# Chunks 0 to 3 of a retention kernel: scaled values, a mask made on the chip, and another order of loads

## The chip, the cores and the metric

One core of a Trainium2 chip runs one program. The metric is the device time of one execution in microseconds (us), as the median of several runs. The profile is one execution with every instruction, semaphore and DMA recorded. TensorE (PE in the profile) multiplies; PEld is its weight load. VectorE is DVE, ScalarE is ACT, GpSimd is POOL. SyncE (SP) only issues DMAs.

## The reference, cut to what matters

Three stages follow one another: retention (a linear attention with decay), a first MLP, and an RMS norm with a gated MLP. Only retention is touched by most of the change.

```
state = gamma * state + k[t]^T v[t]          # per batch and head, 64 x 64
y[t]  = 1/sqrt(64) * q[t] state              # q, k, v: (2, 8, 768, 64)
h = x @ w_in;  x2 = (h * sigmoid(1.702 h)) @ w_out            # (1536, 512), d_ff 2048
xn = x2 / rms(x2) * rms_g;  out = (silu(xn @ w_gate) * (xn @ w_val)) @ w_out2
```

`gamma` is 1 - 2^(-5 - head). `w_in`, `w_out` and the other weights arrive as 64-bit floats and are converted on the chip.

## The kernel before, in words

**Tiles.** The 768 positions of a batch are six chunks of 128, so there are twelve chunks; `CPB` is 4, the chunks of one block of 512 tokens. Tokens are worked through in three blocks of 512. Chunks 0 to 3 are the first block; they are done in an opening that is written out by hand (lines 850 to 965). Chunks 4 to 11 run inside the loop over the sixteen column blocks f of the first MLP (lines 1002 to 1052).

**A chunk.** `score_products` makes k q for all eight heads (two PSUM tiles, even and odd heads). `masks` multiplies them on VectorE with `dm_sb`, a loaded table that holds scale * gamma^(t-s) on and above the diagonal and zero elsewhere. `intra` multiplies the values with the masked scores. `inter` multiplies the state of the chunks before with q times a decay (`prep_q`, on GpSimd, with the loaded table `qd_sb`) into the same PSUM tile y. `update_products` multiplies k times a decay (`prep_k`, on GpSimd, with `sm_sb`) with the values; `decay` (ScalarE) and `add_update` (VectorE) make the next state S. `x_high` (ScalarE) and `x_low` (VectorE) store y as a rounded part and the rest; the MLP's products use three products of such parts (high x high, high x low, low x high).

**Weights.** `load_next` brings half a weight block (512 KB) into one of four buffers; `convert` turns it into 32-bit floats in five steps, which the opening calls one by one as r[0] to r[4] (ScalarE, ScalarE, VectorE, VectorE, VectorE or the end); `split_in` and `split_out` make the high and low parts. `in_proj` makes h of one column block in twelve products of 512 columns; in the opening h0 is made in two groups, 384 columns for chunks 0 to 2 and 128 for chunk 3 (lines 940 and 952). `mlp1_act` is the gate, on ScalarE, with its low part on VectorE.

**What sets the order.** In the opening, `in_order` pins each engine's instructions to the order of the text. Behind it a planner orders each engine's instructions by its own costs, program order being the priority, and may draw instructions forward into the opening. SyncE issues loads in the order of the text (lines 866 to 886); two small ones go out on ScalarE's queue (`sm_sb`, line 871, and `g_sb`, line 882, the norm's factor, which ScalarE later scales on line 1076).

**Near the end of the first MLP**, `set_tasks` gives five steps that make the seven operands of the next stage's products out of a weight block (x, sums, more, y, z); at f = 14 one of them is called for block 0 (line 1024), the others at f = 15.

Of the kernel before, what the change touches and what calls it, by code (L numbers as in the profile page):

```python
# [19 lines left out]
C = 128  # L20
# [7 lines left out]
T = 512  # L28
# [16 lines left out]
HELD = 2  # L45
WARM, MORE = 8, 0
# [7 lines left out]
def tile_retention_mlp_swiglu(  # L54
# [231 lines left out]
    def prep_k(c):  # L286
        t = tmp(f"kd{c}")
        nc.gpsimd.tensor_tensor(
            out=t.rearrange("p (h d) -> p h d", h=H),
            in0=ld["kv", c][:, 0],  # L290
            in1=sm_sb[:, 0:H].to_broadcast([128, H, D]),
            op=ALU.mult,
        )
        at["kd", c] = t
# [17 lines left out]
    def score_products(c, p):  # L312
        t = ld["qk", c]
        sc = at["sc", c] = [psum(p, f"sc{c}_{e}") for e in range(2)]
        begun = len(nc.cur_bb.bb.instructions)
        earlier = of(mybir.EngineType.PE)[-1]
        for n in range(NP):
            for e in range(2):
                nc.tensor.matmul(  # L319
                    out=sc[e][:, n * C:(n + 1) * C],  # L320
                    lhsT=t[64 * e:64 * e + 64, 1, n, :],
                    rhs=t[64 * e:64 * e + 64, 0, n, :],
                    start=True,
                    stop=True,
                )
        if c > CPB:
            after(of(mybir.EngineType.PE, begun)[0], earlier)

    def masks(c):
        sc = at.pop(("sc", c))  # L330
        for e in range(2):
            a = tmp(f"a{c}_{e}")
            nc.vector.tensor_tensor(
                out=a, in0=sc[e], in1=dm_sb[:, e].rearrange("p n c -> p (n c)"), op=ALU.mult
            )
            at["a", c, e] = a
# [11 lines left out]
    def inter(c, p):  # L348
        if c % NC == 0:
            return  # L350
        y, begins = y_of(c, p)
        qd = at.pop(("qd", c))
# [25 lines left out]
    def x_of(c):  # L378
# [8 lines left out]
        return [x[:, :, i * C:(i + 1) * C] for x in xt[j]]  # L387

# [478 lines left out]
    load_mask(0)  # L867
    load_qk(1)
    load_mask(1)
    load_kv(0)  # L870
    nc.scalar.dma_start(out=sm_sb.rearrange("p n o -> p (n o)"), in_=small)
    load_kv(1, (1,))
    nc.sync.dma_start(out=qd_sb.rearrange("p n c -> p (n c)"), in_=qdec)
    load_qk(2)
    load_kv(1, (0,))
    load_kv(2)
    load_qk(3)
    load_next()
    load_kv(3)
    for _ in range(3):  # L880
        load_next()
    nc.scalar.dma_start(out=g_sb, in_=rms_g)
    load_qk(CPB)
    load_kv(CPB)
    load_qk(CPB + 1)
    load_kv(CPB + 1)

    nc.scalar.activation(out=first, in_=ones[:, 0:1], func=ACTF.Silu)
    score_products(0, ps_a)
    score_products(1, ps_a)  # L890
    warming(MORE)
    masks(0)
    prep_k(0)
    intra(0, ps_h)
    masks(1)
    x_high(0)
    intra(1, ps_h)
    update_products(0, ps_t)
    prep(1)
    add_update(0)  # L900
    x_low(0)
    decay(1)

    score_products(2, ps_a)
    inter(1, ps_h)
    update_products(1, ps_t)
    masks(2)
    prep(2)
    x_high(1)
    add_update(1)  # L910
    x_low(1)
    r = convert_next(split=True)
    decay(2)
    r[0]()
    r[1]()

    intra(2, ps_h)
    score_products(3, ps_a)
    masks(3)
    r[2]()  # L920
    inter(2, ps_h)
    update_products(2, ps_t)
    add_update(2)
    prep(3)
# [6 lines left out]
    decay(3)  # L931
    r = convert_next(split=True)
    r[0]()
    r[2]()
    intra(3, ps_h)
    inter(3, ps_h)
    x_high(3)
    ps = psum(ps_a, "h0")
    w = parts.pop(("wi", 0))
    in_proj(ps, w, xt[0], True, 0, T - C)  # L940
    update_products(3, ps_t)
    x_low(3)
    r[1]()
    r[3]()
    r[4]()
    load_next()
    add_update(3)
# [3 lines left out]
    split_in(1)  # L951
    in_proj(ps, w, xt[0], True, T - C, T)
    score_products(CPB, ps_t)
    r[2]()
    r[3]()
    ready = of(mybir.EngineType.DVE)[-1]
    masks(CPB)
    prep_q(CPB)
    tc.add_manual_dep(of(mybir.EngineType.Pool)[-1], ready.name, WAIT, reason="order of issue")
# [42 lines left out]
    for f in range(1, F1):  # L1002
# [14 lines left out]
        if f == F1 - 2:  # L1017
# [6 lines left out]
            some(sets[0], 1)  # L1024
# [349 lines left out]
```

## Time and profile before

| | |
|---|---|
| median of 3 runs | 585.38 us (585.36 to 585.67) |
| the profiled execution | 585.22 us |
| its span, first to last instruction | 583.4 us |
| TensorE busy | 575.7 us (99%) |
| VectorE busy | 450.7 us (77%) |
| ScalarE busy | 365.4 us (63%) |
| GpSimd busy | 24.5 us (4%) |
| granted TensorE clock | 0.999 |
| DMA | 135.11 MB, mean 232 GB/s |

The chain of waits that ended last is made of TensorE to 97% and of DMA to 2%. Busy time of TensorE counts from the first to the modelled end of pipelined products, so a busy TensorE is not one at its peak. A row's idle time stands in brackets with what ended it.

### The profile page before, as it was taken

The page shows a single profiled execution, that of the slowest core. Times are in us where ns is not written, and L with a number is a line of the kernel's source. Part 1 is how long each engine was busy: PE and PEld are TensorE (multiplying, and loading weights), DVE is VectorE, ACT ScalarE, POOL GpSimd, SP SyncE. Part 2 cuts the span into 40 slices and gives each one's busy share as a digit, 9 for nine tenths or more (in the row PEclk, how much of TensorE's full clock was granted, in tenths as well). Part 3 has the DMA queues.
Part 4 walks back from the last instruction along what each step waited for, and adds up shares of the span by engine and source line. Part 5 has one row for each costly group of instructions (what it writes and reads, how often), then busy time and mean ns, then how long its engine had stood idle before and what let it go on. Part 6 is the DMA issues. An engine that isn't in the chain of part 4 may idle for free.

```text
span 583.4 us, 9280 instructions
## 1 busy us (share of the span) xinstructions
PE 575.7 (99%) x3274; PEld 481.1 (82%) x3274; DVE 450.7 (77%) x806; ACT 365.4 (63%) x697; POOL 24.5 (4%) x26
## 2 busy tenths in 40 slices
PE   7999999999999999999999999999999999999997
PEld 5887887888788888878888888988989889988885
DVE  3899998879989888367998998888958676644542
ACT  2878776667687887466647875666645446634442
POOL 3300212100000000000000000000000000000000
PEclk9999999999999999999999999999999999999999
DMA  8999999888369899878744336676414476560412
GB/s 321 408 287 379 391 325 370 276 258 311 115 238 317 285 328 349 306 246 315 290 162 165 108 122 203 200 230 220 163 61 138 145 273 247 201 207 11 152 65 74
DMA packets 48287, 135.11 MB, mean 232 GB/s; under 512 B 5616, under 2 KB 5872, under 8 KB 48240
## 3 DMA queue, kind: packets, MB, share of 16 engines
q1 hardware_dynamic: 47808, 134.37, 66.0%
q8 instruction: 26, 0.43, 0.3%
q14 instruction: 21, 0.17, 0.1%
q10 hardware_dynamic: 432, 0.14, 0.1%
HBM read 98.84 MB, written 35.65 MB: 231 GB/s over the span
## 4 chain that ended last, share of the span: by engine, by line
PE 97%; DMA 2%; ACT 0%; DVE 0%; issue 0%; ACTq 0%
PE acc L444 8%; PE h L467 8%; PE acc L446 7%; PE acc L445 7%; PE o L444 6%; PE o L445 6%; PE o L446 6%; PE sc L319 2%; PE y L356 2%; PE y L369 2%; DMA qk<-in_qk 1%; PE m7a L778 1%; PE v0a L778 1%; PE m0a L778 1%; PE m1a L778 1%; PE g10a L778 1%
## 5 line engine op out<-in xcount | busy, mean ns | idle before, releaser
L445 PE MATMUL o<-w,gh 128*128 128x512 f32 x144 | 56.2, 390 | 0.0
L444 PE MATMUL o<-w,gh 128*128 128x512 f32 x144 | 56.2, 390 | 0.0
L446 PE MATMUL o<-w,gl 128*128 128x512 f32 x144 | 56.1, 389 | 0.0
L201 DVE CUSTOM_DVE_ANT_0 qw<-qw,uw 128x1024 uint16<-128x1024 uint16 x67 | 45.9, 686 | 2.6 <-ACT uw L199 0.5
L198 ACT ACTIVATE qw<-w 128x512 f32<-128x512 f32 x67 | 44.6, 665 | 2.6 <-DMA w<-in_w 2.6
L199 ACT ACTIVATE uw<-w 128x512 uint32<-128x512 uint32 x67 | 44.7, 668 | 0.0
L450 DVE TENSOR_TENSOR gl<-gw,gh 128x512 fp32r<-128x512 f32 x24 | 16.6, 691 | 27.1 <-ACT gh L449 27.0
L200 DVE TENSOR_SCALAR qw<-qw 128x512 uint32<-128x512 uint32 x67 | 28.8, 431 | 9.9 <-ACT qw L198 9.8
L449 ACT ACTIVATE gh<-gw 128x512 fp32r<-128x512 f32 x24 | 15.1, 630 | 28.0 <-PE o L445 22.5
L446 PEld LDWEIGHTS o<-w,gl 128*128 128x128 f32 x144 | 27.0, 188 | 5.7
L445 PEld LDWEIGHTS o<-w,gh 128*128 128x128 f32 x144 | 27.1, 188 | 4.6
L444 PEld LDWEIGHTS o<-w,gh 128*128 128x128 f32 x144 | 27.1, 188 | 4.5
L444 PE MATMUL acc<-gh,wo 128*128 128x512 f32 x64 | 25.9, 412 | 0.0
L446 PE MATMUL acc<-gh,wo 128*128 128x512 f32 x64 | 25.0, 391 | 0.0
L445 PE MATMUL acc<-gl,wo 128*128 128x512 f32 x64 | 25.0, 391 | 0.0
L445 PE MATMUL acc<-gl,wowp 128*128 128x512 f32 x64 | 24.9, 389 | 0.0
L446 PE MATMUL acc<-gh,wowp 128*128 128x512 f32 x64 | 24.9, 389 | 0.0
L444 PE MATMUL acc<-gh,wowq 128*128 128x512 f32 x64 | 24.9, 389 | 0.0
L445 PE MATMUL acc<-gl,wowq 128*128 128x512 f32 x64 | 24.9, 389 | 0.0
L446 PE MATMUL acc<-gh,wowq 128*128 128x512 f32 x64 | 24.9, 389 | 0.0
L207 DVE SCALAR_TENSOR_TENSOR qw<-w,qw 128x512 uint32<-128x512 uint32 x36 | 24.7, 686 | 0.2
L467 PE MATMUL h<-xt0h,wih 128*128 128x512 f32 (+2 forms) x68 | 24.8, 387 | 0.0
(1519 smaller groups left out, 1691.4 us busy)
## 6 DMA issues: line engine op xcount, KB each, us to landing
w<-in_w SPq DMA_DIRECT2D x68, 512.0 KB, 6.2
qk<-in_qk SPq DMA_DIRECT2D x12, 512.0 KB, 7.6
kv<-in_kv SPq DMA_DIRECT2D x10, 512.0 KB, 8.5
gmd<-gm SPq DMA_DIRECT2D x16, 256.0 KB, 4.4
gwm<-gmd SPq DMA_DIRECT2D x16, 256.0 KB, 4.5
g1d<-gs SPq DMA_DIRECT2D x12, 256.0 KB, 2.1
g2d<-gl SPq DMA_DIRECT2D x12, 256.0 KB, 2.6
gw<-g1d SPq DMA_DIRECT2D x12, 256.0 KB, 3.4
```

Source lines behind the costliest of these rows:

```text
L198: lambda: nc.scalar.activation(out=q, in_=high.bitcast(F32), func=ACTF.Copy, scale=2.0 ** -112),
L199: lambda: nc.scalar.activation(out=t, in_=low, func=ACTF.Copy, scale=2.0 ** -29),
L200: lambda: nc.vector.tensor_scalar(out=m, in0=m, scalar1=3, scalar2=None, op0=ALU.logical_shift_left),
L201: lambda: nc.vector.tensor_tensor(out=m, in0=m, in1=t, op=ALU.add),
L207: nc.vector.scalar_tensor_tensor(out=dst, in0=high, scalar=0x80000000, in1=m, op0=ALU.bitwise_and, op1=ALU.bitwise_or)
L444: nc.tensor.matmul(out=out, lhsT=ah, rhs=bh, start=first, stop=False)
L445: nc.tensor.matmul(out=out, lhsT=ah, rhs=bl, start=False, stop=False)
L446: nc.tensor.matmul(out=out, lhsT=al, rhs=bh, start=False, stop=last)
L449: nc.scalar.activation(out=hi, in_=src, func=ACTF.Copy)
L450: nc.vector.tensor_tensor(out=lo, in0=src, in1=hi.bitcast(F32), op=ALU.subtract)
L467: nc.tensor.matmul(out=ps[:, begin:end], lhsT=w[a][:, k * 128:(k + 1) * 128], rhs=x[b][:, k, begin:end], start=begin == 0 and o == order[0 ...
L778: nc.tensor.matmul(out=bank, lhsT=u, rhs=v, start=first and k == 0 and x == 0, stop=k == 1 and x == 2, skip_group_check=True,)
```

## The change

For chunks 0 to 3 the decay is taken apart differently. `prep_k` scales the values instead of k, by gamma^(127 - s), and both `update_products` (k unscaled, values scaled) and `intra` use the scaled values. The mask is then gamma^(-128) per head on and above the diagonal and zero elsewhere: `steps`, filled by eight VectorE fills and two GpSimd selects in a buffer that a later tile of x uses. What is left, scale * gamma^(t+1), is `qd_sb`: for chunks 0 and 1 y is multiplied with it on VectorE before x is taken (`scale_y`), and q is used as loaded; for chunks 2 and 3 q is multiplied with it before the scores, and the same q is used for scores and state.

Other parts: for chunks 0 and 3 three of eight heads of the scaled values are made on ScalarE; the scores of chunk 0 go to four PSUM tiles and are masked in halves; the mask table `dm_sb` is loaded in one piece behind chunk 4's q and k; k and v of chunks 0 to 3 are loaded apart, v first; `g_sb` is loaded last, from SyncE; h0 is made in one group of twelve; `in_proj` takes low weights before low x where it goes by part; the order of the opening is new; at f = 14 three steps of block 0 are called, not one.

```diff
+BY_Y = 2
-    def prep_k(c):
+    def prep_k(c, end=H):
         t = tmp(f"kd{c}")
         nc.gpsimd.tensor_tensor(
-            in0=ld["kv", c][:, 0],
-            in1=sm_sb[:, 0:H].to_broadcast([128, H, D]),
+            out=t.rearrange("p (h d) -> p h d", h=H)[:, 0:end],
+            in0=ld["kv", c][:, int(c < CPB), 0:end],
+            in1=sm_sb[:, 0:end].to_broadcast([128, end, D]),
             op=ALU.mult,
         )
+        for h in range(end, H):
+            nc.scalar.activation(out=t[:, o], in_=ld["kv", c][:, 1, h, :], func=ACTF.Copy, scale=sm_sb[:, h, :])
     def score_products(c, p):
+        q = t[:, 0] if c < BY_Y or c >= CPB else at["qd", c].rearrange("p (n c) -> p n c", n=NP)
+        sc = at["sc", c] = [psum(p, f"sc{c}_{e}") for e in range(2 if c else 4)]
     def masks(c):
+        table = steps if c < CPB else dm_sb
+        step = T if c else T // 2
+        for x, o in enumerate(range(0, T, step)):
+            for e in range(2):
+                nc.vector.tensor_tensor(out=at["a", c, e][:, o:o + step], in0=sc[2 * x + e][:, o:o + step], ...
     def inter(c, p):
+        qd = ld["qk", c][:, 0].rearrange("p n c -> p (n c)") if c < BY_Y else at.pop(("qd", c))
     def intra(c, p):
+                    lhsT=at["kd", c][:, (2 * n + e) * D:(2 * n + e) * D + D] if c < CPB else ld["kv", c][:, 1, 2 * n + e, :],
+    def scale_y(c):
+        t = tmp(f"ys{c}")
+        nc.vector.tensor_tensor(out=t, in0=at["y", c], in1=qd_sb.rearrange("p n c -> p (n c)"), op=ALU.mult)
+        at["y", c] = t
     def update_products(c, p):
+        if c < CPB:
+            kd, vt = ld["kv", c][:, 0].rearrange("p h d -> p (h d)"), kd
     def in_proj(ps, w, x, by_part, begin=0, end=T):
-            order.sort(key=lambda o: (0, 2, 1)[o[1]] if begin == 0 and end < T else o[1])
+            order.sort(key=lambda o: (0, 2, 1)[o[1]])
+    steps = xt_p.tile([128, 2, NP, C], F32, tag="xt1h", name="steps")
+    for e in range(2):
+        for n in range(NP):
+            nc.vector.memset(steps[:, e, n, :], (1.0 - 2.0 ** (-5.0 - (2 * n + e))) ** -C)
+        nc.gpsimd.affine_select(
+            out=steps[:, e], in_=steps[:, e], pattern=[[0, NP], [1, C]], compare_op=ALU.is_ge,
+            fill=0.0, base=0, channel_multiplier=-1,
+        )
```

The new order of loads on SyncE (`sm_sb` alone stays on ScalarE's queue): q and k of 0, q and k of 1, v of 0, v of 1, k of 0, `qd_sb`, q and k of 2, k of 1, q and k of 3, v of 2, k of 2, v of 3, first weights, k of 3, second weights, q and k of 4, `dm_sb`, third and fourth weights, then chunks 4 and 5, `g_sb`.

The new order of the opening, where a name stands for the function and its chunk:

```
scores 0 (ps_a), scores 1 (ps_t), masks 0, prep_k 0 (5 heads on GpSimd), intra 0, masks 1, prep_k 1, update 0,
intra 1, add_update 0, scale_y 0, x_high 0, x_low 0, prep_q 2, decay 1, inter 1, update 1,
scores 2, scale_y 1, add_update 1, prep_q 3, prep_k 2, x_high 1, masks 2, x_low 1, decay 2,
inter 2, scores 3, intra 2, update 2, prep_k 3 (5 heads), masks 3, convert r[0..2], add_update 2, r[3..4], load,
x_high 2, split_in 0, x_low 2, intra 3, inter 3, convert r[0], x_high 3, x_low 3, update 3, h0 (twelve products),
r[1], r[2], decay 3, r[3], add_update 3, r[4], load, split_in 1, convert r[0..1],
scores 4, masks 4, prep_q 4, r[2..4], load, gate of h0, prep_k_by_head 4, split_out 0
```

```diff
@@ f == F1 - 2
-            some(sets[0], 1)
+            some(sets[0], 3)
```

## Rows read from the trace of the kernel before

**Rows 1.** Busy time by stretch: start:end length, PE, PEld, DVE, ACT, POOL, clock, DMA share, GB/s
```profile
4.41:29.40 24.99, 22.23 (x293) 19.07 (x293) 17.03 (x30) 14.75 (x38) 9.54 (x8) 1.00 1.02 399
29.40:60.00 30.60, 30.60 (x240) 24.79 (x240) 28.65 (x52) 25.02 (x50) 2.34 (x2) 1.00 0.97 339
60.00:137.50 77.50, 77.50 (x560) 62.63 (x559) 67.29 (x110) 54.26 (x103) 12.15 (x9) 1.00 0.93 325
...
145.00:160.00 15.00, 15.00 (x67) 11.86 (x66) 14.92 (x24) 10.67 (x18) 0.00 (x0) 1.00 0.35 125
```

**Rows 2.** Timeline of TensorE, opening: start, us, line, operation, [idle before <- what ended it]
```profile
4.41 1.55 PE L319 MATMUL sc<-qk 64*128 64x128 f32 x16
7.25 1.16 PE L319 MATMUL sc<-qk 64*128 64x128 f32 x16 [1.30 <-DMA qk<-in_qk]
8.71 1.10 PE L369 MATMUL y<-a,kv 128*64 128x128 f32 x16 [0.29 <-DVE a L333]
10.05 1.09 PE L369 MATMUL y<-a,kv 128*64 128x128 f32 x16 [0.24 <-DMA kv<-in_kv]
...
12.01 1.16 PE L319 MATMUL sc<-qk 64*128 64x128 f32 x16 [0.40 <-DMA qk<-in_qk]
...
18.93 1.09 PE L369 MATMUL y<-a,kv 128*64 128x128 f32 x16 [0.52 <-DVE S_sb L429]
```

**Rows 3.** Chain of waits, the products of h0 (two groups) and h1: start, us
```profile
21.05 2.28 PE h L467 x12
23.95 1.49 PE h L467 x12
...
26.52 2.94 PE h L467 x12
```

**Rows 4.** Timeline of VectorE in the opening
```profile
6.01 0.69 DVE L333 TENSOR_TENSOR a<-sc,dm_sb 128x512 f32<-128x512 f32 x1 [6.01 <-PE sc L319]
...
11.65 0.42 DVE L431 COPY S_sb<-u 128x256 f32<-128x256 f32 x1 [1.78 <-PE u L413]
```

**Rows 5.** Timeline of GpSimd in the opening
```profile
0.73 0.20 POOL L851 MEMSET ones<- 128x128 f32 x1 [0.29 <-POOLq L1367]
...
9.37 1.04 POOL L288 TENSOR_TENSOR kd<-kv,sm_sb 128x512 f32<-128x512 f32 x1 [8.36 <-DMA kv<-in_kv]
10.65 1.27 POOL L281 TENSOR_TENSOR qd<-qk,qd_sb 128x512 f32<-128x512 f32 x1 [0.24 <-DMA qd_sb<-in_qdec]
12.61 1.04 POOL L288 TENSOR_TENSOR kd<-kv,sm_sb 128x512 f32<-128x512 f32 x1 [0.68 <-DMA kv<-in_kv]
...
18.95 1.43 POOL L288 TENSOR_TENSOR kd<-kv,sm_sb 128x512 f32<-128x512 f32 x1 [1.84 <-DMA kv<-in_kv]
```

**Rows 6.** Timeline of ScalarE in the opening
```profile
6.12 0.21 ACT L1076 ACTIVATE g_sb<-g_sb 128x4 f32<-128x4 f32 x1 [2.77 <-DMA g_sb<-in_rms_g]
...
25.47 0.60 ACT L494 ACTIVATE g<-h 128x512 f32<-128x512 f32 x1 [0.60 <-PE h L467]
...
26.64 2.01 ACT L300 ACTIVATE kd<-kv,sm_sb 128x64 f32<-128x64 f32 x8
```

**Rows 7.** Timeline of VectorE behind the opening
```profile
33.70 0.68 DVE L450 TENSOR_TENSOR wil<-w,wih 128x512 fp32r<-128x512 f32 x1
...
45.10 0.69 DVE L488 SCALAR_TENSOR_TENSOR gl<-g,gh 128x512 fp32r<-128x512 f32 x1
```

**Rows 8.** Timeline of ScalarE behind the opening
```profile
38.93 0.66 ACT L198 ACTIVATE qw<-w 128x512 f32<-128x512 f32 x1 [1.01 <-DMA w<-in_w]
...
43.41 0.58 ACT L494 ACTIVATE g<-h 128x512 f32<-128x512 f32 x1
```

**Rows 9.** Timeline of TensorE behind the opening
```profile
35.22 0.39 PE L467 MATMUL h<-xt0h,wil 128*128 128x512 f32 x1
...
37.26 0.39 PE L467 MATMUL h<-xt0h,wil 128*128 128x512 f32 x1
...
46.72 0.39 PE L445 MATMUL acc<-gl,wo 128*128 128x512 f32 x1
```

More of the change, by code (lines that the diff above doesn't have):

```diff
@@ L313, in score_products @@
         t = ld["qk", c]
-        sc = at["sc", c] = [psum(p, f"sc{c}_{e}") for e in range(2)]
+        q = t[:, 0] if c < BY_Y or c >= CPB else at["qd", c].rearrange("p (n c) -> p n c", n=NP)
+        sc = at["sc", c] = [psum(p, f"sc{c}_{e}") for e in range(2 if c else 4)]
         begun = len(nc.cur_bb.bb.instructions)
@@ L319, in score_products @@
                 nc.tensor.matmul(
-                    out=sc[e][:, n * C:(n + 1) * C],
+                    out=sc[e if c else n // 2 * 2 + e][:, n * C:(n + 1) * C],
                     lhsT=t[64 * e:64 * e + 64, 1, n, :],
-                    rhs=t[64 * e:64 * e + 64, 0, n, :],
+                    rhs=q[64 * e:64 * e + 64, n, :],
                     start=True,
@@ L330, in masks @@
         sc = at.pop(("sc", c))
+        table = steps if c < CPB else dm_sb
         for e in range(2):
[L332 to L336, printed above, removed]
+            at["a", c, e] = tmp(f"a{c}_{e}")
+        step = T if c else T // 2
+        for x, o in enumerate(range(0, T, step)):
+            for e in range(2):
+                nc.vector.tensor_tensor(
+                    out=at["a", c, e][:, o:o + step],
+                    in0=sc[2 * x + e][:, o:o + step],
+                    in1=table[:, e].rearrange("p n c -> p (n c)")[:, o:o + step],
+                    op=ALU.mult,
+                )
     def scores(c, p):
@@ L875, in tile_retention_mlp_swiglu @@
     load_kv(1, (0,))
-    load_kv(2)
     load_qk(3)
+    load_kv(2, (1,))
+    load_kv(2, (0,))
+    load_kv(3, (1,))
     load_next()
-    load_kv(3)
-    for _ in range(3):
+    load_kv(3, (0,))
+    load_next()
+    load_qk(CPB)
+    nc.sync.dma_start(out=dm_sb.rearrange("p e n c -> p (e n c)"), in_=dmask)
+    for _ in range(2):
         load_next()
-    nc.scalar.dma_start(out=g_sb, in_=rms_g)
-    load_qk(CPB)
     load_kv(CPB)
@@ L886, in tile_retention_mlp_swiglu @@
     load_kv(CPB + 1)
+    nc.sync.dma_start(out=g_sb, in_=rms_g)
     nc.scalar.activation(out=first, in_=ones[:, 0:1], func=ACTF.Silu)
     score_products(0, ps_a)
-    score_products(1, ps_a)
+    score_products(1, ps_t)
     warming(MORE)
     masks(0)
-    prep_k(0)
+    prep_k(0, 5)
     intra(0, ps_h)
     masks(1)
+    prep_k(1)
+    update_products(0, ps_a)
+    intra(1, ps_h)
+    add_update(0)
+    scale_y(0)
     x_high(0)
[L897 to L900, printed above, removed]
     x_low(0)
+    prep_q(2)
     decay(1)
+    inter(1, ps_h)
+    update_products(1, ps_a)
     score_products(2, ps_a)
-    inter(1, ps_h)
-    update_products(1, ps_t)
+    scale_y(1)
+    add_update(1)
+    prep_q(3)
+    prep_k(2)
+    x_high(1)
     masks(2)
-    prep(2)
-    x_high(1)
-    add_update(1)
     x_low(1)
+    decay(2)
+    inter(2, ps_h)
+    score_products(3, ps_a)
+    intra(2, ps_h)
+    update_products(2, ps_t)
+    prep_k(3, 5)
+    masks(3)
     r = convert_next(split=True)
-    decay(2)
     r[0]()
     r[1]()
-    intra(2, ps_h)
-    score_products(3, ps_a)
-    masks(3)
     r[2]()
-    inter(2, ps_h)
-    update_products(2, ps_t)
     add_update(2)
-    prep(3)
     r[3]()
@@ L930, in tile_retention_mlp_swiglu @@
     x_low(2)
-    decay(3)
+    intra(3, ps_h)
+    inter(3, ps_h)
     r = convert_next(split=True)
     r[0]()
-    r[2]()
[L935 to L943, printed above, removed]
+    x_high(3)
+    x_low(3)
+    update_products(3, ps_t)
+    ps = psum(ps_a, "h0")
+    in_proj(ps, parts.pop(("wi", 0)), xt[0], True)
+    r[1]()
+    r[2]()
+    decay(3)
     r[3]()
+    add_update(3)
     r[4]()
     load_next()
-    add_update(3)
+    split_in(1)
     r = convert_next(split=True)
@@ L950, in tile_retention_mlp_swiglu @@
     r[1]()
-    split_in(1)
-    in_proj(ps, w, xt[0], True, T - C, T)
     score_products(CPB, ps_t)
+    masks(CPB)
+    prep_q(CPB)
     r[2]()
     r[3]()
[L956 to L959, printed above, removed]
     r[4]()
```

17 lines of the change are left out of this document (7 added, 10 removed).

## The prediction

> **What bounds the kernel now.** I read the busy time by stretch first [rows 1], then TensorE's own timeline of the opening [rows 2], then the engines that feed it [rows 4 to 6], and last the first iterations behind the opening [rows 7 to 9]. The reader is to see in the stretches that from 29.40 us on TensorE is busy for all of 30.60, 77.50 and 15.00 us: nothing stands open there, and a feeder that gets faster behind 29.4 us can give nothing. Between 4.41 and 29.40 us it is busy for 22.23 of 24.99 us. This is the only place that the change can shorten; what it does elsewhere can only cost.
>
> The open time of the opening is in five gaps [rows 2]: 1.30 us until chunk 1's q and k land, 0.29 us until chunk 0's masked scores are there, 0.24 us for chunk 1's values, 0.40 us for chunk 2's q and k, 0.52 us for the state S that chunk 2's update makes. Sum 2.75 us.
>
> Two feeders are nearly full: DMA has a share of 1.02 in the opening and 0.97 from 29.4 to 60 us, and VectorE is busy for 28.65 of 30.60 us there [rows 1]. So a TensorE that is earlier by x meets weights that are not earlier by x. That decides how much of x is kept.
>
> **The change, part by part.** *Landings.* All loads go down one line, and a wait that a load ends tells when it was there. Counted in KB from the line's start: 1,280 (chunk 1's q, k) at 7.25 us [rows 2]; 2,048 (chunk 0's k) at 9.37 and 2,560 (the q decay) at 10.65 [rows 5]; 2,304 at 10.05 and 3,072 at 12.01 [rows 2]; 3,328 at 12.61 and 5,376 (chunk 3's k, v) at 18.95 [rows 5]. From 1,280 to 3,328 KB that is 5.36 us, or 0.67 us for 256 KB. The new line has the same bytes in another order. Chunk 1's q, k are complete at 1,024 KB: 7.25 - 0.67 = 6.6 us. Then v of chunk 0 (1,280 KB, 7.25), v of 1 (7.9), k of 0 (8.6), q decay (9.3), q, k of 2 (10.65), k of 1 (11.3), q, k of 3 (12.6), v of 2 (13.3), k of 2 (13.9), v of 3 (14.6), first weights (15.9), k of 3 (16.6), second weights (5,376 KB, 18.95). The mask table lands behind chunk 4's q, k at 21.6 us (two times 512 KB, 2.68 us, on) and is first read behind 24 us. The third weights go back by one such place, to 23.0 us; by the list below ScalarE reads them from 23.3 us, so I cost that at nothing, with 0.3 us of cover.
>
> *Triangle.* Eight fills of 128 columns on VectorE and two selects of 512 columns on GpSimd, ahead of the first scores. No row shows either. A VectorE copy of 256 columns took 0.42 us [rows 4] and a GpSimd fill of 128 columns 0.20 us [rows 5], so I take 0.25 us a fill: four are done at 1.75 us, eight at 2.75. A select lies between that 0.20 us and the 1.43 us of the longest GpSimd product of 512 columns; I take 1.04 us, its usual time [rows 5]. The selects end at 2.8 and 3.9 us, at the upper bound at 4.6 us. The masks want them at 5.2 us, half way through the first scores. Cost nothing; what happens without that cover is a rival below.
>
> [...]
>
> *Chunk 0.* The first scores still run from 4.41 to 5.96 us. The second start at 6.6 instead of 7.25 and end at 7.75 (1.16 us). The first a x v product has a new wait: beside the masked scores it now needs scaled values, five heads on GpSimd (5/8 of 1.04 = 0.65 us) and three on ScalarE (2.01/8 = 0.25 us each [rows 6]) from 7.25 us: ready at 8.05 us. It had started at 8.71. All of TensorE is queued behind it, so this wait carries the whole advance. The masks of chunk 0, four halves of 0.42 us from 5.2 us, are done at 6.9 and lie beside it.
>
> Gaps so far: 5.96 to 6.6 (0.64) and 7.75 to 8.05 (0.30).
>
> *Chunks 1 to 3.* From 8.05 us I put the products one behind the other in the new order and look for what is late. Update 0 at 9.1 needs k of 0 (8.6). a x v of chunk 1 at 9.7 needs its scaled values (GpSimd 7.95 to 9.0) and masks (9.1). Its state product at 10.7 needs S, copied at 10.2. Update 1 at 11.75 needs k of 1 (11.3): 0.45 us to spare, the tightest load. Scores 2 at 12.35, state product 2 at 13.45 (S at 13.2), scores 3 at 14.5, a x v 2 at 15.55 (scaled values 14.8, masks 14.9), update 2, a x v 3 at 17.2 (masks 16.95), state product 3 at 18.25, update 3 at 19.3 to 19.85. None is late by this list, so the gaps 0.24, 0.40 and 0.52 go too. Two multiplications of y on VectorE (0.69 us each, as the masks) and the longer split masks (4 x 0.42 against 2 x 0.69) add 1.7 us to VectorE, and six heads 1.5 us to ScalarE; until 16 us both had long idle stretches (VectorE 1.78 us before the copy at 11.65 [rows 4]), so I cost them at nothing. GpSimd loses one product of 1.27 us [rows 5].
>
> *h0 in one group.* It must wait for chunk 3's x. y of chunk 3 ends at 19.3; ScalarE has one step of the second weights (there at 18.95) ahead of it, so with 0.60 us for each of the two [rows 6] x is there at 20.15: a new gap of 0.30 us. In return twelve products of 512 columns take 2.94 us, as h1 does, where the two groups took 2.28 and 1.49 us [rows 3]: 0.83 us less.
>
> *Sum of the opening:* 2.75 - (0.64 + 0.30 + 0.30) + 0.83 = 2.34 us. The scores of chunk 4, which followed h0 at 25.44 us (23.95 + 1.49), would start near 23.1. Bounds: 3.58 us with no gap at all (2.75 + 0.83); and 0.58 us if the scaled values took 1.43 us, the longest GpSimd product, in place of 0.65, and h0's weights slipped by 0.98 us more, as the load at 18.95 did against the 0.67 us pace (12.61 + 5.36 = 17.97).
>
> *What the feeders let through.* ScalarE's gate for h0 ran at 25.47 us [rows 6]. In the new order it has ahead of it, from 20.15 us: a step of the second weights (0.6), four state decays (1.0), VectorE's signs of those weights (0.7), their split (0.6) and two steps of the third weights (1.2), and so comes at 24.3 to 24.6. It and VectorE are thus earlier by about 0.9 us, not 2.34, and both are full from there on. Iteration 2's low weights were done at 34.38 us (33.70 + 0.68) [rows 7] and read at 35.22 [rows 9], 0.84 us to spare. New: ready 33.5, wanted 32.9. TensorE gives 0.6 us back: 2.34 - 0.6 = 1.7 us kept.
>
> *The last edit* takes four 256-column sums of VectorE (0.42 us each) one iteration earlier, near 130 us. TensorE has no gap there, so it gains nothing. VectorE is busy for 14.92 of 15.00 us from 145 to 160 us [rows 1]; its bound is a loss of 1.7 us if all four stood ahead of something awaited, and I take zero, since they leave the later, fuller stretch.
>
> The profiled execution had 585.22 us, span 583.4, so 1.8 us lie around the span; the median of the runs is 585.38. Span 581.7, executions 583.5, and beside the median 585.38 - 1.7 = **583.7 us**.
>
> **Rivals.** *A, the old order of ScalarE holds.* In iteration 2 the gate of h2 (its last product ended at 37.65 us [rows 9]) ran only at 43.41 us, behind work that began when a weight load landed at 38.93 [rows 8]; its low part was there at 45.79 (45.10 + 0.69) [rows 7], wanted at 46.72 [rows 9]. The line of loads has the same bytes before that load, so it is not earlier. If the gate stays behind it, only 46.72 - 45.79 = 0.93 us is kept: 584.45 us. For it: DMA share 0.97 there. Against it: that order is the planner's, and with h2 earlier the gate can move ahead.
>
> *B, slower: the norm factor's scaling stands in ScalarE's way.* Its load goes from ScalarE's queue (landed 6.1 us) to the end of SP's, behind chunk 5's k, v: 8,960 KB, or 18.95 + 14 x 0.67 = 28.3 us. The scaling was drawn forward into the opening, where ScalarE stood 2.77 us for it [rows 6]. If the planner puts it before the gate of h0 at 24.6, ScalarE stands for 3.7 us, iteration 2's weights come at 37.2 instead of 33.5, and TensorE wants them at 32.9: 2.34 - 4.3 = -2.0, or 587.4 us. From a stand of about 1.7 us on it decides against the kernel. For it: it happened before; against it: behind 25 us ScalarE has other work ready.
>
> *C, late triangle.* If the second select ends at X, behind 7.3 us, GpSimd's scaled values follow at X + 0.65 and the first a x v product at X + 0.7, in place of 8.05. At X = 9.9 that is 10.6, 2.55 us later, and all of the 2.34 us is gone: 585.6 us. It needs selects of 3.6 us each (9.9 less 2.75, halved), against 1.43 us for the longest product [rows 5]. [...]
>
> *D, all is kept:* the planner moves the low weights of iteration 2 forward too: 585.38 - 2.34 = 583.04 us.
>
> **Chances.** Forecast 0.40 (own range 583.0 to 584.2), A 0.25, B 0.12, C 0.08, D 0.10; 0.05 for a late load somewhere in chunks 1 to 3, which takes about 2 us, to 585.7. What a measurement of this kernel can tell from no change is 0.2%, or 1.17 us: below 584.21 lie the forecast and D, 0.50; above 586.55 lies B and a tail of C and the last case, 0.17; between them 0.33. From 582.8 to 586.6 us leaves out about 0.17 above and little below.
>
> **What would show it.** The first a x v product near 8.05 us and waiting for GpSimd or ScalarE, not for VectorE; TensorE's gaps from 4.4 to 23 us near 1.2 us in sum; twelve h0 products in a row from about 20.15; scores of chunk 4 near 23.1. A gap of some 0.6 us before iteration 2's low-weight products shows the forecast, one near 45 us A; a ScalarE idle until 28 us at the g_sb scaling shows B; a first mask behind 7 us shows C. I am wrong if the opening itself does not get shorter, or if TensorE stands open anywhere behind 60 us.

## The result and the profile after

The changed kernel is slower: 590.19 us (median of 17 runs, 588.51 to 591.11) against 585.65 us for the kernel before beside it (17 runs). The ratio is 1.0057, with a 95% interval of 1.0036 to 1.0077; the medians alone stand 4.54 us or 0.8% apart. The kernel before has a few single runs at 589 to 593 us in each comparison, which enter its ratios and not its median, so the medians are given with each ratio below. The forecast of 583.7 us and its range of 582.8 to 586.6 us both miss. The profiled execution took 591.01 us, with a span of 588.2 us and a mean granted clock of 0.997.

Busy time by stretch of the changed kernel, with the columns of [rows 1]:

```profile
4.41:29.40 24.99, 22.05 (x280) 18.18 (x280) 18.45 (x31) 14.00 (x37) 7.31 (x7) 1.00 1.01 391
29.40:60.00 30.60, 30.50 (x237) 24.13 (x237) 28.93 (x53) 26.37 (x53) 4.19 (x2) 1.00 0.90 326
60.00:90.00 30.00, 30.00 (x226) 24.31 (x225) 26.35 (x41) 20.70 (x45) 5.97 (x4) 1.00 0.95 332
90.00:105.00 15.00, 12.76 (x101) 10.18 (x102) 13.00 (x20) 9.84 (x20) 2.57 (x2) 0.89 0.94 324
105.00:145.00 40.00, 40.00 (x254) 32.58 (x251) 33.04 (x54) 26.59 (x48) 3.79 (x3) 1.00 0.86 293
145.00:160.00 15.00, 14.87 (x65) 11.59 (x64) 13.94 (x23) 11.13 (x20) 0.00 (x0) 1.00 0.42 145
```

Two things are to be seen. The opening is no fuller than before (22.05 of 24.99 us). And from 90 to 105 us, where the kernel before had no gap, TensorE is busy for only 12.76 of 15 us and its clock is 0.89.

**The opening.** TensorE's timeline there (start, us, line, operation, what ended the idle time before it), to be held against [rows 2]:

```profile
7.73 1.09 PE L382 MATMUL y<-a,kd 128*64 128x128 f32 x16 [0.63 <-POOL kd L289]
...
13.50 1.09 PE L369 MATMUL y<-qd,S_sb 64*64 64x128 f32 x16 [0.32 <-DVE S_sb L449]
...
18.79 1.09 PE L369 MATMUL y<-qd,S_sb 64*64 64x128 f32 x16 [0.57 <-DVE S_sb L449]
...
21.71 1.20 PE L487 MATMUL h<-xt0h,wih 128*128 128x512 f32 x4 [1.22 <-ACT xt0h L408]
...
24.82 1.52 PE L326 MATMUL sc<-qk 64*128 64x128 f32 x16
26.45 1.21 PE L487 MATMUL h<-xt0h,wih 128*128 128x512 f32 x4
```

The first a x v product is a whole 0.98 us earlier than in [rows 2]. But four gaps (0.63 + 0.32 + 0.57 + 1.22 = 2.74 us) have taken the place of five with 2.75. Chunk 4's scores start at 24.82 us, 0.54 us earlier than the 25.36 us of the kernel before, and h1 starts at 26.45 us in both: by the end of the opening nothing is gained.

**The stall.** TensorE around chunk 9, with the last product ahead of the gap:

```profile
91.06 1.16 PE L326 MATMUL sc<-qk 64*128 64x128 f32 x16
...
94.78 0.39 PE L466 MATMUL acc<-gh,wo 128*128 128x512 f32 x1
97.40 1.53 PE L369 MATMUL y<-qd,S_sb 64*64 64x128 f32 x16 [2.24 <-DVE a L344]
```

Chunk 9's scores end at 92.2 us, and its masks run on VectorE only at 96.58 us. Before, they ran at 91.61 us, right behind the scores. Behind the gap the granted clock goes to half (0.50 for 1.00) for 3.4 us, from 97.9 to 101.3 us; windows of 2 us, in the columns of [rows 1]:

```profile
96.00:98.00 2.00, 0.60 (x10) 0.63 (x12) 2.00 (x5) 1.31 (x3) 0.00 (x0) 0.98 1.00 402
98.00:100.00 2.00, 2.00 (x22) 1.67 (x20) 1.91 (x4) 2.00 (x5) 0.00 (x0) 0.50 1.04 266
100.00:102.00 2.00, 2.00 (x26) 1.89 (x24) 2.00 (x5) 1.70 (x4) 0.00 (x0) 0.67 0.81 243
102.00:104.00 2.00, 2.00 (x11) 1.61 (x10) 1.78 (x4) 1.59 (x5) 0.00 (x0) 1.00 1.04 424
```

Instruction by instruction, TensorE is 0.65 us later than in the kernel before ahead of the gap (chunk 9's scores at 91.06 us for 90.41), 2.96 us later behind it (97.40 for 94.45), 4.56 us later after the half clock, and 5.1 to 5.2 us from 165 us to the end. So the gap costs 2.3 us, the half clock 1.6, and some 0.6 each is lost ahead and behind. Of the 17 runs, 11 list a mean clock of 0.996 or 0.997 and spans of 587.7 to 588.3 us, the other 6 a clock of 0.999 or 1.000 and spans of 586.4 to 586.8: the difference is about that 1.6 us.

**Why the masks are late.** VectorE in the changed kernel, at three places:

```profile
20.65 1.79 DVE L470 TENSOR_TENSOR wil<-w,wih 128x512 fp32r<-128x512 f32 x1 [0.70 <-ACT wih L469]
...
77.88 1.57 DVE L202 CUSTOM_DVE_ANT_0 qw<-qw,uw 128x1024 uint16<-128x1024 uint16 x1
79.37 1.53 DVE L470 TENSOR_TENSOR wo<-w,wo 128x512 fp32r<-128x512 f32 x1
80.83 0.68 DVE L208 SCALAR_TENSOR_TENSOR w<-w,qw 128x512 uint32<-128x512 uint32 x1
81.43 1.27 DVE L344 TENSOR_TENSOR a<-sc,dm_sb 128x512 f32<-128x512 f32 x2
...
92.48 1.52 DVE L201 TENSOR_SCALAR qw<-qw 128x512 uint32<-128x512 uint32 x1
94.14 1.31 DVE L202 CUSTOM_DVE_ANT_0 qw<-qw,uw 128x1024 uint16<-128x1024 uint16 x1
95.37 0.68 DVE L470 TENSOR_TENSOR wo<-w,wo 128x512 fp32r<-128x512 f32 x1
95.98 0.68 DVE L208 SCALAR_TENSOR_TENSOR w<-w,qw 128x512 uint32<-128x512 uint32 x1
96.58 1.27 DVE L344 TENSOR_TENSOR a<-sc,dm_sb 128x512 f32<-128x512 f32 x2
```

The same forms take 0.69 us (0.42 for L201) elsewhere. And GpSimd, where every long row above has a product beside it:

```profile
1.56 1.22 POOL L885 TENSOR_SCALAR_AFFINE_SELECT steps<-steps 128x512 f32<-128x512 f32 x2 [0.49 <-DVE steps L884]
...
20.62 1.27 POOL L282 TENSOR_TENSOR qd<-qk,qd_sb 128x512 f32<-128x512 f32 x1 [3.79 <-PE u L433]
...
77.45 1.45 POOL L282 TENSOR_TENSOR qd<-qk,qd_sb 128x512 f32<-128x512 f32 x1 [10.80 <-DMA w<-in_w]
78.86 1.49 POOL L289 TENSOR_TENSOR kd<-kv,sm_sb 128x512 f32<-128x512 f32 x1
92.34 1.38 POOL L282 TENSOR_TENSOR qd<-qk,qd_sb 128x512 f32<-128x512 f32 x1 [11.98 <-DMA w<-in_w]
93.68 1.23 POOL L289 TENSOR_TENSOR kd<-kv,sm_sb 128x512 f32<-128x512 f32 x1
```

Each of the lengthened VectorE operations above starts inside a GpSimd product and ends 0.3 to 0.6 us after that product does: the product of 77.45 us ends at 78.90, the operation begun at 77.88 ends at 79.45. It ends as if it had waited for nearly the whole product and then run. I call that a lock; it costs 0.6 to 1.1 us each time here. In the kernel before, the second product of chunk 8 met the masks instead; VectorE, then GpSimd:

```profile
77.67 1.01 DVE L450 TENSOR_TENSOR wil<-w,wih 128x512 fp32r<-128x512 f32 x1 [0.70 <-ACT wih L449]
78.60 1.27 DVE L333 TENSOR_TENSOR a<-sc,dm_sb 128x512 f32<-128x512 f32 x2
...
91.61 1.28 DVE L333 TENSOR_TENSOR a<-sc,dm_sb 128x512 f32<-128x512 f32 x2
...
93.24 1.53 DVE L488 SCALAR_TENSOR_TENSOR gl<-g,gh 128x512 fp32r<-128x512 f32 x1
```

```profile
76.80 1.32 POOL L281 TENSOR_TENSOR qd<-qk,qd_sb 128x512 f32<-128x512 f32 x1 [11.84 <-DMA wo6d<-wo]
78.09 1.49 POOL L288 TENSOR_TENSOR kd<-kv,sm_sb 128x512 f32<-128x512 f32 x1
```

The masks read their scores from PSUM and are not lengthened (two in 1.27 us beside a product that runs from 78.09 to 79.58 us). The operations of the changed kernel's long rows, on SBUF operands, lost 0.63 to 1.10 us each time; in the kernel before the one at 77.67 us lost 0.32 and the one at 93.24 us 0.84.

The loser can also be GpSimd. Chunk 5's query product in the changed kernel:

```profile
39.30 3.15 POOL L282 TENSOR_TENSOR qd<-qk,qd_sb 128x512 f32<-128x512 f32 x1 [17.41 <-PE sc L326]
```

It started while VectorE was in the middle of a row of operations on SBUF operands, one right behind the other, and took 3.15 us where the same form takes 1.27 at 10.69 us. VectorE's operations kept their 0.68 us until a mask came at 41.22 us, and only the one begun at 41.81 was lengthened (0.92 us for 0.42).

### The profile page after: what moved, and what is told of

It reads as the page before. It is cut to its first block, busy times and chain, and to the rows that moved or that the text cites. A ratio compares the mean times of both kernels' runs of the same rounds, so it can differ in the third digit from the quotient of the medians.

```text
span 588.2 us, 9288 instructions
## 1 busy us (share of the span) xinstructions
PE 578.2 (98%) x3262; PEld 481.5 (82%) x3262; DVE 457.3 (78%) x818; ACT 366.5 (62%) x703; POOL 25.5 (4%) x27
## 4 chain that ended last, share of the span: by engine, by line
PE 84%; DMA 5%; DVE 4%; ACT 4%; issue 2%; SPq 0%; DVEq 0%; ACTq 0%
PE acc L464 6%; PE acc L465 6%; PE acc L466 6%; PE o L465 6%; PE o L466 6%; PE o L464 6%; PE h L487 4%; DMA w<-in_w 1%; DMA wo4d<-wo 1%; DMA wo5d<-wo 1%; DMA kv<-in_kv 1%; PE m7a L798 1%; PE v0a L798 1%; PE g6a L798 1%; PE g10a L798 1%
## 5 line engine op out<-in xcount | busy, mean ns | idle before, releaser
L202 DVE CUSTOM_DVE_ANT_0 qw<-qw,uw 128x1024 uint16<-128x1024 uint16 x67 | 47.3, 707 | 3.5 <-ACT uw L200 0.5
L201 DVE TENSOR_SCALAR qw<-qw 128x512 uint32<-128x512 uint32 x67 | 29.9, 448 | 8.7 <-ACT qw L199 8.6
L487 PE MATMUL h<-xt0h,wih 128*128 128x512 f32 x64 | 24.4, 397 | 1.3 <-ACT xt0h L408 1.2
```

Of the source, the lines that this page charges most:

```text
L201: lambda: nc.vector.tensor_scalar(out=m, in0=m, scalar1=3, scalar2=None, op0=ALU.logical_shift_left),
L202: lambda: nc.vector.tensor_tensor(out=m, in0=m, in1=t, op=ALU.add),
L487: nc.tensor.matmul(out=ps[:, begin:end], lhsT=w[a][:, k * 128:(k + 1) * 128], rhs=x[b][:, k, begin:end], start=begin == 0 and o == order[0 ...
```

## The experiments

All times of before in these comparisons are medians of 586.19 or 586.21 us, and every variant was timed in 6 to 12 runs.

**1. The wait of chunk 4's decayed query, put back.** The change also takes out a wait of GpSimd, which neither the prediction nor the list of the change's parts mentions; the product of 20.62 us above can start early because of it.

```diff
+    ready = of(mybir.EngineType.DVE)[-1]
     masks(CPB)
     prep_q(CPB)
+    tc.add_manual_dep(of(mybir.EngineType.Pool)[-1], ready.name, WAIT, reason="order of issue")
```

> One part undone: chunk 4's q product on GpSimd waits again for VectorE's instruction ahead of chunk 4's masks, as in the kernel before. Theory (GpSimd's two-input product locks VectorE's two-input operation): the 1.79 us of h0's low weights at 20.65 us falls to 0.69, h1 starts some 0.5 us earlier, the weights' conversions are 0.5 to 1.1 us earlier all along, and with them the masks of chunk 9 that TensorE waited 2.24 us for; time 588 to 589.5 us. Rival (the opening is late by its loads alone, the later gap has a cause of its own): the 1.79 us stay or go, but h1 starts at 26.4 and the 2.24 us gap stays; time 590.2 us.

588.34 us, ratio 1.0019 (0.9987 to 1.0050): 2.15 us above the median of before, where the changed kernel stood 4.54 above. The two medians are not of like runs: 4 of these 10 runs list a clock of 0.997, 11 of the changed kernel's 17 one of 0.996 or 0.997. Among runs at 0.999 or 1.000 the median span falls from 586.6 to 585.5 us, among the others from 588.1 to 587.35: the wait is worth 0.8 to 1.1 us. The lock at 20.65 us is gone and h1 starts at 25.77 us instead of 26.45. The stall stays, since the masks and TensorE both come 1.0 us earlier:

```profile
96.43 1.31 PE L369 MATMUL y<-qd,S_sb 64*64 64x128 f32 x16 [2.25 <-DVE a L344]
```

So this wait explains a part, and the stall has a cause of its own.

**2. Iteration 9's second conversion by steps**, as iteration 4's is: its first two steps where they were, its three others behind the masks.

```diff
-            if f == JOIN and count["converted"] == 2 * f + 3:
+            if f in (JOIN, 9) and count["converted"] == 2 * f + 3:
```

> The changed kernel with one thing more: at f = 9 the second weight conversion's VectorE steps stand behind chunk 9's masks, as the kernel already does at f = 4. Theory (TensorE's 2.24 us at 97.4 us are VectorE's order: masks behind two conversions, and the half clock of 97.9 to 101.3 us follows from that gap): gap and half clock both go, granted clock 1.00 from 5 us to the end, 590.2 - 2.2 - 1.6 = 586.4 us. Rival (all feeders are late, so a gap of the same size opens elsewhere): 589 us or more, with a gap of about 2 us at another place. A second rival (the clock falls by itself): gap gone, half clock stays: 588 us.

586.23 us, ratio 0.9982 (0.9951 to 1.0012): 0.04 us above the median of before. The masks come 2.63 us earlier, and there is no gap and a clock of 1.000:

```profile
93.95 1.28 DVE L344 TENSOR_TENSOR a<-sc,dm_sb 128x512 f32<-128x512 f32 x2
```

Nearly the whole loss is that stall with what follows it.

**3. Chunk 9's products on GpSimd earlier**, so that they don't run just ahead of its masks (without the wait of experiment 1).

```diff
         prep(c)
+        if c == 9:
+            return
         tc.add_manual_dep(...)
```

> The changed kernel, but GpSimd's two products of chunk 9 no longer wait for its scores, so they run when their data are there, some 10 us ahead. Theory (in the 2.24 us gap, 1.10 + 0.63 us are VectorE locked out by these two GpSimd products): the two VectorE operations ahead of the masks take 0.42 and 0.68 us, the gap shrinks to about 0.5 us, the half clock goes or shortens; 587 to 588 us. Rival (late weights alone make the gap): the gap stays near 2 us; 590 us.

589.97 us, ratio 1.0053 (1.0029 to 1.0078): missed, and the number is the rival's. The products ran at 86.54 and 88.32 us and locked two other conversions there (1.78 and 1.53 us); the masks came at 96.65 us, the gap was 2.5 us. A lock 6 us further ahead of the masks cost them as much as one just ahead. This run alone leaves the rival standing, that late weights make the gap; experiment 9 decides.

**4. Both repairs, and `x_high(3)` ahead of the second conversion's first step** on ScalarE.

```diff
+    x_high(3)
     r[0]()
-    x_high(3)
```

> The changed kernel with the wait for chunk 4's q product back, the conversion at f = 9 behind the masks, and x of chunk 3 on ScalarE ahead of the second weights' first step. Theory: h0 starts 0.55 us earlier (21.15 in place of 21.71 us), h1 about 1 us earlier than 26.45, no gap at chunk 9, no half clock: 585.0 to 585.8 us, no faster than the kernel before by more than 0.5 us. Rival (feeders are late whatever the opening does): h1 earlier, but gaps of 1 to 2 us between 33 and 100 us; 587 us or more.

585.54 us, ratio 0.9966 (0.9939 to 0.9993), as expected. h0 at 21.07 us (gap 0.67), chunk 4's scores at 24.06 us, 1.3 us earlier than before; behind iteration 2's low weights some 0.5 us of it is left.

**5. Both repairs alone.**

> The changed kernel with both repairs: the wait of chunk 4's decayed query on GpSimd is put back, and the second conversion of iteration 9 is put in by steps, so that chunk 9's masks run ahead of its later halves. Without the reordered x_high of the run that also had that. Theory that the two faults are separate and add (a locked VectorE in the opening, worth some 0.5 to 1 us at the first step of iteration 1, and the stall at 94.8 us with the half clock behind it, worth 4 us): neither shows in the trace, the time is 585.4 to 585.9, that is within 0.2% of the kernel before. Rival that moving x_high ahead of the second conversion was what made the best run fast: scores of chunk 4 start at 24.6 us instead of 24.06 and the whole is at 586.2, no faster than with the joining alone.

585.36 us, ratio 0.9966 (0.9936 to 0.9996). The repairs add, and the earlier `x_high` is worth nothing: with its h0 at 21.52 us this kernel is as fast. By the medians it is 0.85 us or 0.15% faster than before, less than a measurement of this kernel tells apart with certainty. Part of that is the clock: all its 12 runs list 0.999 or 1.000, and so do 11 of the 35 runs of before, whose median is 585.78 us, 0.42 above it. In the two profiles nothing is won: TensorE is 0.57 us ahead of the kernel before from 41 to 137 us, level with it from 166 us on, and starts its last product at 578.96 us in both. It is the best version that computes everything.

**6. The last edit undone** in the kernel of experiment 4.

```diff
-            some(sets[0], 3)
+            some(sets[0], 1)
```

> The best kernel so far (wait put back, iteration 9 joined, x_high early) with the last edit of the change undone: one step of the first mixing weights' halves in iteration 13 instead of three. I had priced that edit at nothing. Theory that it is not nothing: in the trace of the best run 0.55 us of lead over the kernel before is still there at 139 us and gone at 160 us, the stage that this edit reorders; with one step as in the kernel before the lead stays and the time is 584.9 to 585.2. Rival that the lead is lost to something else there (the missing m-steps of the order, the conversions' own pace): the time stays at 585.5, within 0.2.

586.95 us, ratio 0.9999 (0.9973 to 1.0024): 1.4 us more than experiment 4, so neither expectation held. TensorE now waits where the kernel before did not; groups of its instructions from 138 to 162 us (busy us, mean ns | idle before, and what ended it):

```profile
L464 PE MATMUL acc<-gh,wowp 128*128 128x512 f32 x8 | 2.4, 420 | 0.8 <-ACT gh L507 0.7
...
L798 PE MATMUL m0a<-xmh,wm0yl 128*128 128x512 f32 x4 | 1.7, 418 | 0.2 <-DVE wm0yl L470 0.2
```

From 146 to 160 us TensorE is busy for 13.04 of 14.00 us, where experiment 4 has 13.90. From 128 to 160 us the open time is 1.16 us, against 0.10 in experiment 4. The sums of block 0 that the edit moves ran on VectorE from 138.57 us, behind four 1,024-column operations; with three steps they run from 132.90, in the kernel before (with one) from 135.89. So the planner's order makes the edit matter: here one step called at iteration 14 puts those sums later than it did before. With three steps TensorE still loses its lead of some 0.5 us in this stage (experiments 4 and 5); what takes it stays open.

**7. Control: the kernel before with iteration 9 joined.**

> Control: the kernel before with only the joining at iteration 9. In its trace chunk 9's masks run right behind their scores (91.57 and 91.61 us), so there is no stall to take away. Theory that the joining only repairs what the change brought about: no difference, 585.4 to 585.9. Rival that the joining is a gain of its own, which the change has nothing to do with: 584.5 to 585.0, and then the repaired kernels owe it part of their time.

586.33 us, ratio 1.0000 (0.9979 to 1.0021). The joining is a repair and no gain of its own. (In its profile TensorE waits 0.56 us for chunk 8's masks, ahead of the joining; behind that its distance to the kernel before stays at 0.8 us.)

**8. The kernel before without the wait of experiment 1.**

> The kernel before with only the wait of chunk 4's decayed query taken out (it is one of the edits of the change, and the prediction did not price it). Theory: that wait kept GpSimd's product of two SBUF operands off the time in which VectorE makes the low half of weight 1; without it the product starts when the query lands (23.9 us or so), VectorE's subtraction of about 0.7 us takes up to 1.8, and the time rises by 0.3 to 1.0 us, to 586.0 to 586.7. Rival: in this kernel the query lands late enough that the product falls beside other work; nothing changes, 585.6 within 0.3.

587.04 us against 586.21; the ratio of 1.0005 (0.9976 to 1.0034) tells nothing, the trace does. The product ran at 24.02 us for 1.60 us, and VectorE's combining beside it took 1.65 us instead of 0.69:

```profile
24.52 1.65 DVE L207 SCALAR_TENSOR_TENSOR w<-w,qw 128x512 uint32<-128x512 uint32 x1
26.10 0.41 DVE L429 TENSOR_TENSOR S_sb<-u,S_sb 128x256 f32<-128x256 f32 x1
```

The state S behind it was late for TensorE: chunk 4's scores, which began 0.30 us later than in the kernel before, went on 0.98 us later (third product at 26.56 us for 25.58), and from 30 us on TensorE stays 1.2 us behind. So the lock costs 0.9 us. The price is as expected; the operation hit was the combining, and not the low half of weight 1.

**9. GpSimd's products of chunks 8 and 9 left out** (their undecayed q and k are used, so a part of the computation is missing), with the wait of experiment 1.

```diff
+        if c in (8, 9):
+            at["qd", c] = ld["qk", c][:, 0].rearrange("p n c -> p (n c)")
+            at["kd", c] = ld["kv", c][:, 0].rearrange("p h d -> p (h d)")
+            return
```

> The changed kernel with the wait of chunk 4's query put back, and with GpSimd's two products of chunk 8 and of chunk 9 left out (their undecayed q and k are used instead, so part of the computation is missing). Question: why chunk 9's masks come 4.0 us later than in the kernel before. Theory of the locks: between 60 us and those masks VectorE lost 4.3 us to GpSimd's products of two SBUF operands (rows lengthened by 0.85, 0.88, 0.84, 1.10 and 0.63 us), where the kernel before lost 1.2; without the products of chunks 8 and 9 3.45 us of it go, the masks stand at about 92.5 us, TensorE's idle time ahead of chunk 9's state product is under 0.6 us (it was 2.3), no stretch at half clock follows, and the time is 586.2 to 586.7. Rival that the conversions are late by their own order: the idle time stays above 1.5 us and the time at 587.4 or more.

584.94 us, ratio 0.9959 (0.9934 to 0.9984). VectorE at the two chunks' masks:

```profile
78.61 1.28 DVE L344 TENSOR_TENSOR a<-sc,dm_sb 128x512 f32<-128x512 f32 x2
...
92.62 1.28 DVE L344 TENSOR_TENSOR a<-sc,dm_sb 128x512 f32<-128x512 f32 x2
```

The masks stand where the theory put them (92.5 us), no wait of TensorE behind 60 us is left, and the profile's mean clock is 1.000. The time fell below the expected range. Without the four locks there is no stall, so they make it; late weights alone do not.

**10 and 11. The products behind the masks**: for chunks 8 and 9 (with the wait of experiment 1), and for chunks 5 to 11 in the kernel of experiment 5.

```diff
-        made = of(mybir.EngineType.PE)[-1]
+        made = of(mybir.EngineType.DVE if c in (8, 9) else mybir.EngineType.PE)[-1]
```

> The changed kernel with the wait of chunk 4's query put back, and for chunks 8 and 9 GpSimd's products wait for the second mask of their chunk on VectorE instead of for its scores on TensorE. Nothing is left out. Theory: the locks then fall behind the masks, as at 63.97 and 93.24 us in the kernel before; the masks of chunk 9 come 3.4 us earlier than with the products ahead of them, the idle time of 2.3 us and the half clock behind it go, 586.2 to 586.8, as long as the state product, which waits for the decayed query, finds it in time. Rival: the query is now what comes last; TensorE waits for GpSimd instead of VectorE by 1 to 2 us, and the time is 587.5 to 588.5.

589.23 us, ratio 1.0028 (1.0001 to 1.0055): the rival's wait, and a time above its range. Masks at 92.93 us, unlocked, with nothing left out, but the decayed query was then the last to come. The profile's mean clock is 0.996, and 9 of the 12 runs list 0.996 or 0.997, with spans of 587.1 to 587.8 us; the other three have 585.3 or 585.4. TensorE's waits (us in total, times, longest):

```profile
PE y L369 <- POOL qd L282: 2.2, 1, 2.2
```

> The kernel with both repairs (wait put back, iteration 9 joined), and for chunks 5 to 11 GpSimd's products wait for the second mask of their chunk instead of for its scores. If locks ahead of masks still cost TensorE anything there, it is faster than 585.36 us by 0.2 to 0.6; my expectation is no difference, 585.2 to 585.6, since TensorE shows no wait behind 60 us in the kernel with both repairs. If a decayed query is late anywhere it shows as a wait for GpSimd and the time rises by that wait.

592.83 us, ratio 1.0105 (1.0069 to 1.0141): the same wait, three times with 5.5 us in all, 4.4 of them in one, and a mean clock of 0.997 in the profile.

**12. One pair of ScalarE's instructions in the old order** (with the wait of experiment 1): in iteration 6, weight 15's conversion ahead of the high half of block 6's output weights.

```diff
+        made = of(mybir.EngineType.Activation)[-1]
+        half = len(nc.cur_bb.bb.instructions)
         split_out(f)
+        if f == 6:
+            after(of(mybir.EngineType.Activation, half)[0], made)
```

> The changed kernel with the wait of chunk 4's query put back and one pair of ScalarE's instructions in the order that the kernel before has: in iteration 6 the two conversion steps of weight 15 run ahead of the high half of block 6's output weights, which waits for VectorE. In the changed kernel ScalarE stood 2.95 us for that half at 64.6 to 67.6 us, while weight 15 had landed at 64.8 us and was converted at 68.1; in the kernel before it was converted at 64.4. Theory: this order, another choice of the planner behind another opening, is where the conversions fall behind by 1.8 us; in time again, they let GpSimd's products of chunk 8 meet the masks, which read PSUM, instead of two conversions; chunk 9's masks come at 92.5 us or earlier instead of 95.6, TensorE's wait of 2.25 us for them and the half clock behind it go, and the time is 585.3 to 586.2. Rival: the conversions are late by more than this pair (the locks come anyway, or the weights' loads are late): the wait stays above 1.5 us and the time at 587.4 or more.

(The times that this expectation names are those of experiment 1.) 587.12 us, ratio 1.0009 (0.9986 to 1.0031): 1.2 us less than experiment 1, but the rival was nearer. Weight 15 was converted at 65.21 us and VectorE stood 1.1 of the 1.84 us earlier at 75 us; the locks came all the same. VectorE, then TensorE:

```profile
76.45 1.78 DVE L470 TENSOR_TENSOR wo<-w,wo 128x512 fp32r<-128x512 f32 x1
78.15 1.53 DVE L208 SCALAR_TENSOR_TENSOR w<-w,qw 128x512 uint32<-128x512 uint32 x1
...
94.96 1.27 DVE L344 TENSOR_TENSOR a<-sc,dm_sb 128x512 f32<-128x512 f32 x2
```

```profile
95.78 1.09 PE L369 MATMUL y<-qd,S_sb 64*64 64x128 f32 x16 [1.74 <-DVE a L344]
```

The planner's order of this pair gave a part of the lag, and 0.5 us of TensorE's wait. Most of the 1.2 us is the clock: all 12 runs list 0.999 or 1.000, with a median span of 585.4 us, and experiment 1's six runs at 1.000 have one of 585.5. Which edit of the opening made the planner choose it, and where the rest of the lag comes from, stays open.

## Why the prediction was wrong, point by point

**What held.** Fills and selects of the triangle (0.90 to 2.05 and 1.56 to 2.78 us) cost nothing: the first select started 0.08 us behind the last fill that it needs. So rival C fell; the 9.9 us that it takes for the end of the second select was an assumption of mine that no run shows, and that select ended at 2.78 us. From chunk 1's v to chunk 2's k (7.93 to 13.87 us) the landings were within 0.1 us of the forecast. The first a x v product waited for GpSimd, as forecast, and came at 7.73 us for 8.05. Rival B fell too: the norm factor's scaling ran at 39.56 us (34.09 in experiment 4), and ScalarE did not wait for it. A could not show in the changed kernel, which had no lead to lose; in experiment 4 nothing was given back near 45 us, where A put it, and D fell too, since not all of the lead was kept.

**The first gaps: near the forecast by luck.** The gap of 0.63 us is not the 0.64 of the sum. That one was to be the wait for chunk 1's q and k, which landed at 5.69 us (forecast 6.6), ahead of the end of chunk 0's scores: no gap there. The 0.63 us are the wait for the scaled values, forecast at 0.30. The pace of 0.67 us for 256 KB does not hold at the head of the line: the half mask table that the change takes out there had stood for 1.55 us (4.36 to 5.92 us in the kernel before).

**"None is late" in chunks 1 to 3: wrong by 0.9 us.** Chunk 3's v landed at 15.94 us (forecast 14.6) and the first weights at 17.24 (15.9). The line had slipped by 1.4 us behind 13.87. The slip of about 1 us that I knew from the kernel before, and left on the second weights, does not belong to a load: there it fell between 16.38 and 18.80 us. In both traces a packet of the instruction queue (16 KB, 1.1 us) lies at that place, begun at 13.36 and 15.84 us; that it makes the slip is not shown. VectorE, for the two gaps:

```profile
11.16 1.35 DVE L414 TENSOR_TENSOR xt0l<-ys,xt0h 128x512 fp32r<-128x512 f32 x1 [0.70 <-ACT xt0h L408]
...
13.04 0.41 DVE L449 TENSOR_TENSOR S_sb<-u,S_sb 128x256 f32<-128x256 f32 x1
...
17.97 0.43 DVE L192 TENSOR_SCALAR qw<-qw 128x512 uint32<-128x512 uint32 x1 [0.90 <-ACT qw L190]
18.31 0.42 DVE L449 TENSOR_TENSOR S_sb<-u,S_sb 128x256 f32<-128x256 f32 x1
```

On VectorE the update's sum at 18.31 us stood behind a conversion step of those weights that waited for them: gap 0.57. Chunk 2's state product waited 0.32 us for a sum that stood behind a `scale_y` and a lengthened `x_low` (1.35 us, beside GpSimd's query of chunk 2). The change itself had opened `x_low` to the lock: `scale_y` puts y into SBUF, where in the kernel before `x_low` read it from PSUM and took 0.68 us beside a product (15.27 us, the product from 14.84 to 15.88). I had costed VectorE's 1.7 us at nothing because it was idle before; it is idle in the sum, not at the moment.

**h0: 1.22 us for 0.30.** ScalarE had the late first weights and then the second weights' step ahead of chunk 3's x. With the forecast gaps 2.34 us were to come out; 2.74 us of gaps in place of 1.24 leave 0.84. h0's products took 3.11 us (21.71 to 24.82) in place of 2.94, because the weight load of the last four waited 0.3 us for `x_low`, which stood behind the locked operation; that leaves 0.67, against 0.54 measured. Without the lock h0 takes 2.94 us and the lead at chunk 4's scores is 0.68 us in experiment 1, 0.86 in experiment 5.

**The removed wait: not in the sum.** It let the query of chunk 4 run beside VectorE's low half of weight 0 (1.79 us for 0.69). Worth 0.9 us by experiment 8's trace and by the medians of experiments 2 and 5.

**What the feeders let through: right as a mechanism, too short in reach.** Experiment 4 shows it: of 1.2 us of lead at 28 us, 0.6 to 0.7 is given back around iteration 2's low weights. That this is the 0.6 of the forecast is luck: the low weights were done at 34.54 us (forecast 33.5) and TensorE wanted them at about 34.0 (forecast 32.9), both about 1.1 us later. And I followed the feeders only to there: "what it does elsewhere can only cost", I wrote, and put that cost at nothing without looking for it. This is the step that failed. Behind another opening the planner gives the loop's conversions another order and pace, they come to chunk 8 2.8 us later on VectorE (1.8 with the wait of experiment 1 put back), and GpSimd's products, which follow TensorE's scores, meet two conversions instead of the masks. From 60 us to chunk 9's masks VectorE then loses 4.3 us to locks, against 1.2 before; that is the stall of 2.24 us and the half clock, 3.9 us in the trace (experiments 2 and 9 are without both). None of my rivals had it; my sentence that I am wrong if TensorE stands open behind 60 us did.

**The last edit: priced at zero, worth 1.4 us in the change's favour** (experiment 6, in the repaired kernel). So it is no part of the loss. I had seen that the sums would leave a fuller stretch, and priced that at nothing because TensorE had no gap there. That was so in the kernel before, where one step put them at 135.89 us; behind the new opening it puts them at 138.57.

## What to carry to other kernels

Behind a planner that orders a full feeder, a shift of TensorE was not carried along as a shift here (of 1.2 us at 28 us in experiment 4, 0.6 to 0.7 was given back around iteration 2's low weights): ask of such a shift which operations it will newly lay side by side, above all VectorE's on SBUF operands beside GpSimd's products (0.63 to 1.10 us each time in the changed kernel's rows), and whether the result that is awaited stands ahead of or behind that meeting. A wait that a kernel carries between two engines without any data between them is a term of the sum when it is removed: look for what it kept apart.

## What the runs showed of the hardware that I had not expected

GpSimd's product of two SBUF operands lengthened four different VectorE operations (0.42 and 0.69 us alone) to as much as 1.52 to 1.79 us, and masks from PSUM not at all (two in 1.27 us). At 39.30 us, where VectorE's operations stood close behind one another, the product was the one to wait (3.15 us for 1.27). In the profiles TensorE waited 2.24, 2.25, 2.5 and 2.2 us at chunk 9 (the changed kernel, experiments 1, 3 and 10), and their mean clock is 0.997, 0.997, 0.997 and 0.996; in the changed kernel half clock (0.50) followed the wait for 3.4 us, worth 1.6 us, and 11 of its 17 runs list the lower mean clock. With the wait of 1.74 us in experiment 12's profile the mean clock is 0.999, TensorE's products of 512 columns behind it took 0.39 to 0.50 us as ahead of it, and all its 12 runs list 0.999 or 1.000. Two GpSimd selects of 512 columns took 1.22 us together, about as long as one product of that size (1.04 and 1.27 us alone).
